# High and low halves turned by one DMA, a head pair's query and key loaded together, row maxima split before they are turned

## The chip, the cores and the metric

The kernel runs on one core of a Trainium2 chip. A core has TensorE (PE; its weight loads are PEld), VectorE (DVE), ScalarE (ACT), GpSimd (POOL) and SyncE (SP), which here issues every DMA; sixteen DMA engines move the data. The metric is the device time of one execution in microseconds, as a median of several executions.

## The reference

Two layers, each an attention with a compressed memory over four segments, and an MLP with a spatial gate. B = 1, S = 2048, D = 640, 32 heads of 20, segments of 512, MLP width 864:

```
def attention(x, wq, wk, wv, wo, beta):        # per head; g = sigmoid(beta)
    for s in range(4):
        p = softmax(q[s] @ k[s].T * 20**-0.5 + causal_mask)
        a_mem = (phi(q[s]) @ M) / (phi(q[s]) @ z + 1e-6)
        o[s] = g * a_mem + (1 - g) * (p @ v[s])
        M, z = M + phi(k[s]).T @ v[s], z + phi(k[s]).sum()
    return o @ wo                              # phi(t) = t + 1 if t > 0 else exp(t)

def mlp(x, w_in, w_sp, b_sp, w_out):
    z = gelu(x @ w_in)
    z1, z2 = z[:, :864], layernorm(z[:, 864:])
    return (z1 * (w_sp @ z2 + b_sp[:, None])) @ w_out

for _ in range(2):
    x = x + attention(layernorm(x), ...)
    x = x + mlp(layernorm(x), ...)
```

## The kernel before

Precision: every operand of a large matmul is split into two 16-bit parts, high (h) and low (l, the rest), and a product is h·h + h·l + l·h. TensorE wants its stationary operand with the contraction on the partitions, so most operands are turned: a DMA transpose turns a tile of 128 rows, one for h and one for l.

A layer has three stages. **phase1a** is attention. **phase1b** takes each of the 16 row tiles (128 rows) through the output projection (where attention has not done it already), the layer norm and both halves of w_in. **phase2** takes each of 16 row tiles of w_sp: `rows` scales and splits it and turns it, `spatial` multiplies it with z2 (96 matmuls at L380), gates, and splits and turns the result u, `tail` multiplies that with w_out (L409).

phase1a handles 64 pairs of heads (16 pairs in each of 4 segments), three slots of time for each. TensorE's order there is written out by hand: `run` goes through the slots and calls, in this order, `fetch`, `combine`, `scores`, the posted small work, `pvs`, `maxes`, `cast`, and then the dense work that is due (`value`, `unit`, `project`, `update`, `read`). The order of the other engines and of the SP queue is set by a scheduler, which goes by its own estimates; each engine, and the SP queue, then works strictly in its order.

What the change touches, in the order in which a pair meets it:

- `prep` loads a row tile, normalises it, and `split_t` (L217) makes h on ScalarE and l (here on GpSimd) and turns each, L222 and L223, into the tiles xth and xtl.
- `unit` computes the query and key rows of 128 columns; `out` splits them, and `stack` (L764, L765) writes them to DRAM, query and key in tensors of their own (stq, stk), each with three rows per dimension (h, l and one of them again). `keys` turns the key features (pkh, pkl, L701) for `update`.
- `fetch` (L777) loads a pair, four slots ahead of its scores by LF and two pairs by LM: query rows into one of five tiles qs, key rows into one of five kb, for each of two heads, four DMAs a pair.
- `scores` multiplies keys and queries twice. First, two pairs ahead, with queries as rows (mp), only to find each row's maximum (L831, `mx`, 128 x 2 x 4); later with keys as rows (es), from which ScalarE makes the exponentials P (L824). es and mp each have one buffer in PSUM, so the next es waits for P and the next mp for mx.
- `maxes` brings the maximum of each row into the query tile, as two more rows of its contraction: TensorE turns mx (L850, mtp, 32-bit), ScalarE scales it to 16 bits (L852, rows 0 to 7 of mr), VectorE takes the rest (L854, rows 32 to 39), and four DMAs (L859) write one row each. mtp lies in the pool "ms" with one buffer, which `update` (mup, L747 to L749) and `read` (num, L720, L724) use too: they wait until mtp's last reader is done.
- `combine` writes the outputs of a unit as h and l to DRAM (L904); `load_o` (L615) and phase1b's `load` (L262) load and turn them.

## Time and profile before

| | us |
|---|---|
| median of 3 runs | 2553.9 (2552.26 to 2554.67) |
| the profiled execution's own time | 2549.18 |
| its span | 2547.5 |

The profile's page gives this busy time over the whole span:

```profile
PE 2272.7 (89%) x21706; PEld 1365.3 (54%) x21706; DVE 1480.9 (58%) x2806; ACT 1146.8 (45%) x1398; POOL 903.1 (35%) x713
```

and in 40 slices of 63.7 us, in tenths, TensorE's, VectorE's, ScalarE's and GpSimd's busy share:

```profile
PE   4778787889899989999978878879998999999998
...
DVE  8677777677654454444335776767775544444431
ACT  4367676677643232211124766657774322112210
POOL 2166566678621000000023666757775110000000
```

Slices 1 to 11 and 21 to 31 are the two attentions: there all four engines work side by side. Behind them TensorE is at nine tenths or more nearly throughout. A row of a group of instructions reads: line, engine, operation, output<-inputs, shapes, count | busy us, mean ns | idle us before them and who ended it. "SPq" is SyncE's queue of DMA issues.

### The profile page before, as it was taken

To read this page: it belongs to the slowest core of one execution; us is meant where nothing else is said; L and a number is where in the kernel's file an instruction comes from. 1 tells how busy PE (TensorE), PEld (TensorE's weight loads), DVE (VectorE), ACT (ScalarE), POOL (GpSimd) and SP (SyncE) were. 2 spreads that over 40 slices of the span, in tenths; PEclk is the share of its full clock that TensorE was granted. 3 is DMA by queue.
4 is the path that set the end of the run, shared out by engine and by line. 5 is a ranking of instruction groups with operands and counts; after the bars stand their busy time and mean duration, and the time that the engine had idled before them with its cause. 6 is when DMAs were issued, how large, how long until landed. Compare 5 with 4: busy or idle time off the path is not lost. (4 is left out here: it accounts for less than half of the span.)

```text
span 2547.5 us, 53964 instructions
## 1 busy us (share of the span) xinstructions
PE 2272.7 (89%) x21706; PEld 1365.3 (54%) x21706; DVE 1480.9 (58%) x2806; ACT 1146.8 (45%) x1398; POOL 903.1 (35%) x713
## 2 busy tenths in 40 slices
PE   4778787889899989999978878879998999999998
PEld 2345454656555545555544445546565555555555
DVE  8677777677654454444335776767775544444431
ACT  4367676677643232211124766657774322112210
POOL 2166566678621000000023666757775110000000
PEclk9899899999999999999989999989999999999999
DMA  6533554323565397767542343343346335776652
GB/s 182 167 106 95 149 132 100 92 77 103 137 175 108 98 263 196 163 155 168 118 95 80 86 104 91 87 104 83 89 108 166 104 87 147 194 178 168 147 139 68
DMA packets 522189, 325.28 MB, mean 128 GB/s; under 512 B 423057, under 2 KB 468241, under 8 KB 516817
## 3 DMA queue, kind: packets, MB, share of 16 engines
q1 hardware_dynamic: 521936, 321.82, 50.1%
q8 instruction: 170, 2.79, 0.4%
q14 instruction: 83, 0.67, 0.1%
HBM read 148.26 MB, written 85.34 MB: 92 GB/s over the span
## 5 line engine op out<-in xcount | busy, mean ns | idle before, releaser
L842 POOL TENSOR_TENSOR PL<-P,PH 128x1280 f16<-128x1280 f32 x248 | 650.9, 2626 | 359.4 <-ACT PH L841 320.9
L831 DVE TENSOR_REDUCE mx<-mp 128x2 f32<-128x1024 f32 (+3 forms) x512 | 409.5, 821 | 181.4 <-PE mp L787 177.8
L824 ACT ACTIVATE P<-es,sc 128x1024 f32<-128x1024 f32 (+1 forms) x384 | 371.6, 968 | 270.2 <-PE mp L787 244.3
L841 ACT CAST PH<-P 128x1280 f16<-128x1280 f32 x256 | 321.2, 1255 | 9.6 <-PE pv L873 2.4
L380 PEld LDWEIGHTS <-wth 128*128 128x128 f16 x2048 | 200.4, 98 | 178.9 <-DMA wth<-wnh 7.9
L380 PE MATMUL gp<-zh,wth 128*128 128x432 f16 x1024 | 271.0, 346 | 7.5 <-DMA wth<-wnh 7.5
L380 PE MATMUL gp<-zh,wtl 128*128 128x432 f16 x1024 | 270.6, 346 | 1.1 <-DMA wtl<-wnl 1.1
L380 PE MATMUL gp<-zl,wth 128*128 128x432 f16 x1024 | 270.9, 346 | 0.0
L815 PE MATMUL es<-qs,kb 64*128 64x512 f16 (+3 forms) x1024 | 150.0, 311 | 70.7 <-ACT P L824 50.9
L383 ACT ACTIVATE u<-gp,bsp,un 128x864 f32<-128x864 f32 x32 | 34.2, 1070 | 391.5 <-PE gp L380 389.8
L208 POOL TENSOR_TENSOR lnrs<-lnve,mhalf 128x1 f32<-128x1 f32 x96 | 58.5, 617 | 427.9 <-DVE lnve L207 404.5
L396 POOL MEMSET unh<- 128x32 f16 x32 | 4.0, 125 | 548.4 <-DMA uh<-unh 513.9
L815 PE MATMUL mp<-kb,qs 60*128 60x512 f16 (+3 forms) x1024 | 144.8, 307 | 50.5 <-DVE mx L831 47.2
L298 PEld LDWEIGHTS <-th 128*128 128x128 f16 x1280 | 125.2, 98 | 109.2 <-DMA th<-xnh 1.4
L356 DVE TENSOR_REDUCE am<-wr 128x1 f32<-128x2048 f32 x32 | 73.2, 2286 | 169.9 <-DMA wr<-in_B_w_sp_dram 169.9
L873 PE MATMUL pv<-vs,PH 128*128 128x41 f16 x2560 | 169.7, 184 | 0.0
L873 PE MATMUL pv<-vs,PL 128*128 128x41 f16 x2560 | 166.0, 182 | 1.6 <-POOL PL L842 1.6
L815 PEld LDWEIGHTS <-kb 64*128 64x128 f16 x1024 | 48.9, 94 | 213.9 <-issue 188.3
L787 PEld LDWEIGHTS <-big 64*128 64x128 f16 x4096 | 142.0, 96 | 39.9 <-issue 5.0
L873 PEld LDWEIGHTS <-PH 128*128 128x128 f16 x2560 | 142.8, 97 | 21.1 <-ACT PH L841 0.2
L366 ACT ACTIVATE wnh<-wr,ivw 128x1024 f16<-128x1024 f32 x64 | 72.0, 1145 | 176.4 <-DVE ivw L361 104.7
L380 PEld LDWEIGHTS <-wtl 128*128 128x128 f16 x1024 | 100.0, 98 | 88.1 <-DMA wtl<-wnl 1.8
(197 smaller groups left out, 4891.0 us busy)
## 6 DMA issues: line engine op xcount, KB each, us to landing
wr<-in_B_w_sp_dram SPq DMA_DIRECT2D x32, 1024.0 KB
x<-x SPq DMA_DIRECT2D x56, 320.0 KB
qs<-stq SPq DMA_DIRECT2D x256, 60.0 KB
kb<-stk SPq DMA_DIRECT2D x256, 60.0 KB
z<-z SPq DMA_DIRECT2D x32, 432.0 KB
cz<-z SPq DMA_DIRECT2D x32, 432.0 KB
xt<-in_A_x_dram SPq DMA_DIRECT2D x32, 320.0 KB
stq<-qhl SPq DMA_DIRECT2D x40, 256.0 KB
```

The costliest lines, as they stand in the source:

```text
L208: nc.gpsimd.tensor_tensor(rs, ve, g.mhalf, ALU.pow)
L298: nc.tensor.matmul(zp[:, n, :FHH], a[:, k, :], b[:, k, c:c + FHH], start=(k == 0 and j == 0), stop=(k == KD - 1 and j == 2))
L356: nc.vector.tensor_reduce(am, wr, AX.X, ALU.max, apply_absolute_value=True)
L366: nc.scalar.activation(hn, wr[:, c], AF.Identity, scale=ivw)
L380: nc.tensor.matmul(gp[:, n, :FHH], a[:, k, :], b[:, k, n * FHH:(n + 1) * FHH], start=(k == 0 and j == 0), stop=(k == NT - 1 and j == 2))
L787: nc.tensor.matmul(out[:, o + c.start:o + c.stop], g.big[r, 64 - 64 * s:192 - 64 * s], g.mask[nm][r, m], start=False, stop=s == 1, skip_gr ...
L815: nc.tensor.matmul(out[:, h, o:o + w], a[r, ac], b[r, bc], start=o == 0, stop=False, skip_group_check=True)
L824: nc.scalar.activation(P[:, :, 512 * c:512 * c + ew], es[:, :, :ew], AF.Exp, scale=g.esc)
L831: nc.vector.tensor_reduce(self.mx[m][:, :, i], mp[:, :, o:o + w], AX.X, ALU.max)
L841: nc.scalar.copy(PH, P[:, h])
L842: (nc.gpsimd if h == 0 or n < self.N - self.TAIL else nc.vector).tensor_tensor(PL, P[:, h], PH, ALU.subtract)
L873: nc.tensor.matmul(pv[:, i, h, :], x[:, c:c + 128], v[:, j, h0 + h, :], start=(j == 0 and x is PH), stop=(j == i and x is PL), skip_group_ ...
```

## The change

Wherever h and l were two tiles and two transposes, they are one tile with a dimension of two and one transpose of twice the columns: in `split_t`, `keys`, `load_o`, `load`, phase2's `rows` and `spatial`. The outputs lie in DRAM as (row, h/l, column), so that both can be turned by one DMA. Query and key rows lie in one DRAM tensor, side by side in each row, and one tile qk holds both: `fetch` issues one DMA a head. VectorE splits the maxima into h and l (mh, 16 columns) right after the last reduction of a pair; TensorE turns both with one 16-bit matmul against a 16-bit identity; ScalarE copies the 16 rows; two DMAs write two rows each.

```
-def split_t(g, h, l, th, tl, src, low=None):
+def split_t(g, hl, t, src, low=None):
-    nc.scalar.copy(h, src)
-    (low or nc.vector).tensor_tensor(l, src, h, ALU.subtract)
-    nc.sync.dma_start(th, h, transpose=True)
-    nc.sync.dma_start(tl, l, transpose=True)
+    nc.scalar.copy(hl[:, 0], src)
+    (low or nc.vector).tensor_tensor(hl[:, 1], src, hl[:, 0], ALU.subtract)
+    nc.sync.dma_start(t.rearrange("p i k c -> p (i k) c"), hl.rearrange("p i c -> p (i c)"), transpose=True)
...
-                for o, n in ((wth, hn), (wtl, ln)):
-                    nc.sync.dma_start(o[:, 8 * i:8 * i + 8, :], n, transpose=True)
+                nc.sync.dma_start(wt[:, i].rearrange("p l k c -> p (l k) c"), hl.rearrange("p l c -> p (l c)"), transpose=True)
...
-            for o, n in ((uh, hn), (ul, ln)):
-                nc.gpsimd.memset(n[:, FH:], 0.0)
-                nc.sync.dma_start(o, n, transpose=True)
+            nc.gpsimd.memset(hl[:, :, FH:], 0.0)
+            nc.sync.dma_start(ut.rearrange("p l k c -> p (l k) c"), hl.rearrange("p l c -> p (l c)"), transpose=True)
...
+    g.ident16 = cp.tile([128, 128], F16, tag="ident16", name="ident16")
+    nc.vector.tensor_copy(g.ident16, g.ident)
...
-        for i in range(2):
-            nc.sync.dma_start(o[:, i], self.o_d[i][t // 4][(t % 4) * 128:(t % 4 + 1) * 128, :], transpose=True)
+        d = self.o_d[t // 4][(t % 4) * 128:(t % 4 + 1) * 128]
+        nc.sync.dma_start(o.rearrange("p i k c -> p (i k) c"), d.rearrange("p i c -> p (i c)"), transpose=True)
...
-            self.pk = [self.u1.tile([128, 4, 128], F16, tag="pk" + p, name="pk" + p) for p in "hl"]
-            for i, o in enumerate(self.pk):
-                nc.sync.dma_start(o, hl[:, i], transpose=True)
+            self.pk = self.u1.tile([128, 2, 4, 128], F16, tag="pk", name="pk")
+            nc.sync.dma_start(self.pk.rearrange("p i t c -> p (i t) c"), hl.rearrange("p i c -> p (i c)"), transpose=True)
...
-        rows = self.st[nm][s % 2][128 * m:128 * m + 128]
+        rows = self.st[s % 2][128 * m:128 * m + 128, :, i]
...
-        for nm, t in (("q", self.qs[n % self.NQ]), ("k", self.kb[n % self.NK])):
-            d = self.st[nm][n // 16 % 2]
-            for h in range(2):
-                c = 40 * (n % 16) + 20 * h
-                self.nc.sync.dma_start(t[64 * h:64 * h + 60], d[c:c + 20].rearrange("p l c -> (p l) c"))
+        for h in range(2):
+            c = 40 * (n % 16) + 20 * h
+            self.nc.sync.dma_start(self.qk[n % self.NQK][64 * h:64 * h + 60], self.st[n // 16 % 2][c:c + 20].rearrange("p l i c -> (p l) i c"))
...
             for i, o, w in red:
                 nc.vector.tensor_reduce(self.mx[m][:, :, i], mp[:, :, o:o + w], AX.X, ALU.max)
+            if c == 2:
+                mx = self.mx[m]
+                mh = self.mh[m] = self.pl2.tile([128, 2, 2, 4], F16, tag="mh", name="mh")
+                nc.vector.tensor_scalar(mh[:, :, 0], mx, -1.0 / MS, None, ALU.mult)
+                nc.vector.scalar_tensor_tensor(mh[:, :, 1], mx, -1.0 / MS, mh[:, :, 0], ALU.mult, ALU.subtract)
...
-        nc.tensor.transpose(tp, mx.rearrange("p h i -> p (h i)"), g.ident)
-        mr = self.pl2.tile([40, 128], F16, tag="mr", name="mr")
-        nc.scalar.mul(mr[0:8], tp, -1.0 / MS)
-
-        nc.vector.scalar_tensor_tensor(mr[32:40], tp, -1.0 / MS, mr[0:8], ALU.mult, ALU.subtract)
-        q = self.qs[n % self.NQ]
-        for i in range(2):
-            for h in range(2):
-                r = 64 * h + 60 + i
-                nc.sync.dma_start(q[r:r + 1, :].rearrange("o (t c) -> o t c", t=4), mr[32 * i + 4 * h:32 * i + 4 * h + 4])
+        tp = self.pm.tile([128, 512], F32, tag="ms", name="mtp")[:16, :128]
+        nc.tensor.matmul(tp, self.mh.pop(n).rearrange("p h i t -> p (h i t)"), g.ident16, start=True, stop=True)
+        mr = self.pl2.tile([16, 128], F16, tag="mr", name="mr")
+        nc.scalar.copy(mr, tp)
+        for h in range(2):
+            r = 64 * h + 60
+            nc.sync.dma_start(self.qk[n % self.NQK][r:r + 2, 0].rearrange("i (t c) -> i t c", t=4), mr[8 * h:8 * h + 8])
```

The SP queue in layer 0's attention, about two pairs where the last outputs of segment 2 (4x160) are written; qs and kb are query and key tiles, o the outputs that are loaded and turned. Before:

```order
L859 DMA qs_347<-mr 1x4x128 x4
L777 DMA qs_351<-stq 60x512 x2
L904 DMA oh_2<-ohl 128x4x160
L777 DMA kb_356<-stk 60x512 x2
L904 DMA ol_2<-ohl 128x4x160
L615 DMA_TRANSPOSE o<-oh_1 128x5x128
L859 DMA qs_348<-mr 1x4x128 x4
L641 DMA x_0_3<-x_9465 128x640
L777 DMA qs_347<-stq 60x512 x2
L777 DMA kb_352<-stk 60x512 x2
L615 DMA_TRANSPOSE o<-ol_1 128x5x128
```

The same place of the changed kernel:

```order
L855 DMA qk_349<-mr 2x4x128 x2
L772 DMA qk_353<-st 60x1024 x2
L900 DMA o_2<-ohl 128x4x160 x2
L613 DMA_TRANSPOSE o<-o_1 128x10x128
L855 DMA qk_350<-mr 2x4x128 x2
L639 DMA x_0_3<-x_9307 128x640
L772 DMA qk_349<-st 60x1024 x2
```

The order is the same; 21 issues became 12.

VectorE in the same attention, one pair's three slots; mx are the reductions (of the slots one, two, one), mr<-mtp the second reader of the turned maxima, ohl and x the outputs and the projection. Before:

```order
L698 SCALAR_TENSOR_TENSOR phl<-phk,sc,phl 128x512
L639 SCALAR_TENSOR_TENSOR x_6015<-yps,sc,xt 128x320
L831 TENSOR_REDUCE mx<-mp 128x2
L901 SCALAR_TENSOR_TENSOR ohl<-oat,ohl 128x480
L831 TENSOR_REDUCE mx<-mp 128x2
L884 TENSOR_TENSOR rs<-pv,iomg 128x8
L639 SCALAR_TENSOR_TENSOR x_6015<-yps,sc,xt 128x320
L885 RECIPROCAL rs<-rs 128x8
L889 TENSOR_TENSOR ab<-pv,rs 128x328
L854 SCALAR_TENSOR_TENSOR mr<-mtp,mr 8x128
L831 TENSOR_REDUCE mx<-mp 128x2 x2
```

The same place of the changed kernel:

```order
L696 SCALAR_TENSOR_TENSOR phl<-phk,sc,phl 128x512
L637 SCALAR_TENSOR_TENSOR x_5911<-yps,sc,xt 128x320
L826 TENSOR_REDUCE mx<-mp 128x2
L830 TENSOR_SCALAR mh<-mx 128x2x4
L831 SCALAR_TENSOR_TENSOR mh<-mx,mh 128x2x4
L897 SCALAR_TENSOR_TENSOR ohl<-oat,ohl 128x480
L826 TENSOR_REDUCE mx<-mp 128x2
L880 TENSOR_TENSOR rs<-pv,iomg 128x8
L637 SCALAR_TENSOR_TENSOR x_5911<-yps,sc,xt 128x320
L881 RECIPROCAL rs<-rs 128x8
L885 TENSOR_TENSOR ab<-pv,rs 128x328
L826 TENSOR_REDUCE mx<-mp 128x2 x2
```

The read of mtp behind ab is gone; two operations stand right behind the pair's last reduction, which mtp now waits for.

A third place, one pair later on VectorE in the changed kernel, where the statistics of a loaded row tile (lnst<-xt) come between:

```order
L826 TENSOR_REDUCE mx<-mp 128x2
L205 BN_STATS lnst<-xt 128x6 x2
L830 TENSOR_SCALAR mh<-mx 128x2x4
L206 BN_AGGR lnmv<-lnst 128x2
L831 SCALAR_TENSOR_TENSOR mh<-mx,mh 128x2x4
L207 TENSOR_SCALAR lnve<-lnmv 128x1
```

Over the program, of the 128 pairs 75 have nothing between the last reduction and the second of these two operations, 33 one operation, and 20 two to five.

More of the change, by code (lines that the diff above doesn't have):

```diff
@@ L284, in xn_t @@
         def xn_t(xn):
-            th = pe2.tile([128, KD, 128], F16, tag="th", name="th")
-            tl = pe2.tile([128, KD, 128], F16, tag="tl", name="tl")
-            h, l = [pe1.tile([128, D], F16, tag="xn" + p, name="xn" + p) for p in "hl"]
-            split_t(g, h, l, th, tl, xn)
-            return th, tl
+            th = pe2.tile([128, 2, KD, 128], F16, tag="th", name="th")
+            hl = pe1.tile([128, 2, D], F16, tag="xnhl", name="xnhl")
+            split_t(g, hl, th, xn)
+            return th[:, 0], th[:, 1]
         def w_in_half(i, th, tl):
@@ L377, in spatial @@
             for k in range(NT):
[L378 removed]
+                for j, (a, b) in enumerate(((0, zh), (0, zl), (1, zh))):
                     for n in range(2):
[L380 removed]
+                        nc.tensor.matmul(gp[:, n, :FHH], wt[:, k // 8, a, k % 8, :], b[:, k, n * FHH:(n + 1) * FHH],
                                          start=(k == 0 and j == 0), stop=(k == NT - 1 and j == 2))
@@ L509 @@
 class Attention:
-    NQ = NK = 5
+    NQK = 5
     LM = 2
@@ L551, in setup @@
         self.po = pool("apo", 1, space=PSUM)
-        self.qs = [sk.tile([128, L], F16, name=f"qs{i}") for i in range(self.NQ)]
-        self.kb = [sk.tile([128, L], F16, name=f"kb{i}") for i in range(self.NK)]
+        self.qk = [sk.tile([128, 2, L], F16, name=f"qk{i}") for i in range(self.NQK)]
         self.vs = [p.tile([128, 4, H, 2 * DH + 1], F16, name=f"vs{i}") for i, p in enumerate((av, sk))]
@@ L740, in update @@
         g, nc = self.g, self.nc
-        pkh, pkl = self.pk
+        pkh, pkl = self.pk[:, 0], self.pk[:, 1]
         n = len(TH[m])
@@ L1063, in rows @@
         return [a[0, t * 128:(t + 1) * 128, :] for t in range(NT)]
-    g.st = {n: [dram(f"st{n}{i}", (D, 3, L), F16) for i in range(2)] for n in "qk"}
+    g.st = [dram(f"st{i}", (D, 3, 2, L), F16) for i in range(2)]
     x = rows(x)
@@ L1068, in interleaved_layers @@
         i = f"_{layer}"
-        o_d = [[dram(f"o{p}{i}_{n}", (L, D), F16) for n in range(NSEG)] for p in "hl"]
+        o_d = [dram(f"o{i}_{n}", (L, 2, D), F16) for n in range(NSEG)]
         x1_d = [dram(f"x1{i}_{t}", (128, D)) for t in range(NT)]
```

62 lines of the change are left out of this document (30 added, 32 removed).

## The prediction

> **What bounds the kernel now.** I read the windows first (the span cut into the stages of both layers), then TensorE's waits, then the chain that ended last, then single pairs in the timeline. The columns of the windows are the length, then busy time of each engine with its instructions, the granted clock, the DMA share and GB/s.
>
> ```profile
> span 2547.5 us, 53964 instructions
> ```
>
> ```profile
> 31.00:717.00 686.00, 571.93 (x7557) 360.54 (x7558) 490.39 (x934) 441.73 (x563) 423.46 (x277) 0.93 0.45 118
> 717.00:908.00 191.00, 189.38 (x1069) 104.36 (x1068) 97.93 (x197) 61.33 (x69) 18.71 (x29) 1.00 0.55 137
> 908.00:1298.00 390.00, 381.06 (x2252) 220.29 (x2251) 168.12 (x293) 75.64 (x74) 11.87 (x41) 0.99 0.71 171
> 1298.00:1962.00 664.00, 554.07 (x7511) 352.27 (x7510) 446.50 (x843) 431.21 (x546) 416.05 (x273) 0.94 0.38 98
> 1962.00:2134.00 172.00, 172.00 (x983) 95.66 (x980) 81.22 (x171) 49.79 (x57) 18.37 (x29) 1.00 0.40 104
> 2134.00:2547.00 413.00, 399.88 (x2333) 229.06 (x2330) 168.10 (x291) 74.22 (x71) 5.58 (x35) 0.99 0.64 152
> ```
>
> The rows are attention, first MLP half (phase1b) and second (phase2) of layer 0, then the same of layer 1. Outside attention TensorE is full: it idles 1.6, 8.9, 0 and 13.1 us there, so transposes and loads that get cheaper in those stages gain almost nothing. In attention it idles 114 and 110 us, and no engine is full. TensorE's order there is written out by hand, so each wait delays all behind it. The whole run's waits of TensorE (total, times, longest):
>
> ```profile
> PE es L815 <- ACT P L824: 50.9, 71, 3.8
> PE mp L815 <- DVE mx L831: 47.2, 43, 3.2
> PE mup L747 <- DVE mr L854: 36.7, 22, 4.6
> PE num L720 <- DVE mr L854: 26.0, 27, 3.2
> PE es L815 <- DMA qs<-mr: 18.2, 21, 3.2
> ```
>
> Three of the five belong to the row maxima: 62.7 us wait until VectorE's L854 has read the turned maxima and the one "ms" bank is free, 18.2 us until the DMAs of L859 have put them into the query tile. The chain that ended last, in attention of layer 1, has the same names among its costs, and L859's issues on the SP queue beside them:
>
> ```profile
> by line: issue 6.7%; DVE mx L831 5.3%; PE kps L661 5.2%; PE pv L873 5.1%; ACT PH L841 4.8%; PE qps L661 4.5%; PE es L815 4.1%; DMA qs<-mr 3.8%; PE vps L600 3.7%; ACT P L824 3.7%; PE num L720 3.1%; PE mp L815 3.0%; PE yps L633 2.9%; POOL PL
> ```
>
> 3.8% of 626 us are 24 us for the landing of the maxima in one layer.
>
> **The maxima, the largest part.** Two places show what goes. In the first, rows of ACT, DVE, TensorE and the SP queue:
>
> ```profile
> 416.83 0.27 PE L850 MATMUL mtp<-ident,mx 128*8 128x128 f32 x1
> 416.94 0.38 PE L661 MATMUL qps<-xth,wql 128*128 128x512 f16 x1
> 417.15 0.38 PE L661 MATMUL kps<-xth,wkh 128*128 128x512 f16 x1
> ...
> 423.16 0.28 PE L747 MATMUL mup<-vs,pkh 128*128 128x147 f16 x1 [4.58 <-DVE mr L854]
> ```
>
> ```profile
> 418.61 0.26 ACT L852 ACTIVATE mr<-mtp 8x128 f16<-8x128 f32 x1
> ```
>
> ```profile
> 421.21 0.89 DVE L205 BATCH_NORM_STATS2 lnst<-xt 128x6 f32<-128x320 f32 x2 [3.48 <-DMA xt<-in_A_x_dram]
> ...
> 422.82 0.28 DVE L854 SCALAR_TENSOR_TENSOR mr<-mtp,mr 8x128 f16<-8x128 f32 x1
> 423.13 0.96 DVE L831 TENSOR_REDUCE mx<-mp 128x2 f32<-128x768 f32 x1
> ```
>
> ```profile
> 423.06 2.53 SPq L859 DMA_DIRECT2D qs<-mr  x4
> ```
>
> ScalarE had read the bank by 418.87; VectorE stood on a load and read it at 422.82 to 423.10. After the change ScalarE is the bank's only reader, so the update of memory would start 4.2 us sooner. But the same VectorE queue holds the maximum at 423.13, which TensorE needs a slot later: a long wait is mostly moved, not removed. The short waits, where VectorE is only the 0.28 us and a handover behind ScalarE, have less of that behind them. Bounds: at least 0.31 us for each of the 49 waits, 15 us; at most all 62.7 us. **I take 30**, nearer the lower end because of rows like 423.13.
>
> The four DMAs take 2.53 us of the SP queue (0.63 each); the last of two leaves 1.3 us sooner, and the first starts with ScalarE's end, at least 0.31 us sooner. The 21 waits of 18.2 us average 0.87 us, less than 1.6, so most vanish; bounds 0 (if two-row writes land later by as much) and 18.2: **15**.
>
> The Trainium skill, DMA: Bandwidth & Descriptors, section "Why a DMA increments its semaphore by 16 and not by 1", says that a DMA runs on the largest number up to 16 that divides the slowest dimension of both sides. By it a write of two rows from eight partitions uses two of the DMA engines where one row from four used four, and the 15 would shrink by what the longer landing takes; no row of before shows such a write.
>
> TensorE's own turn, its readers and two of VectorE's smallest operations:
>
> ```profile
> L854 DVE SCALAR_TENSOR_TENSOR mr<-mtp,mr 8x128 f16<-8x128 f32 x128 | 35.8, 280 | 19.9 <-ACT mr L852 16.2 <-DMA qs<-stq 1.1
> L850 PE MATMUL mtp<-ident,mx 128*8 128x128 f32 x128 | 35.3, 276 | 0.0
> ...
> L884 DVE TENSOR_TENSOR rs<-pv,iomg 128x8 f32<-128x8 f32 x128 | 20.0, 156 | 12.9 <-PE pv L873 12.9
> ```
>
> The next matmul starts 0.11 us after mtp (416.83 to 416.94); the 16-bit matmul of 512 columns behind it holds the array 0.21 us (to 417.15), so one of 128 should hold it 0.05: 128 x 0.05 = **6 us** saved, bounds 0 and 14. The Trainium skill, Perfetto Trace Analysis, section "Transposes", speaks against this edit: logical transposes should be transposes, not standard matmuls, which the new mtp is. By that rule the 6 us would be 0 or a small loss; the trace has no such matmul against an identity to set beside it.
>
> VectorE loses 128 x 0.28 = 36 us and the 16.2 us in which L854 stood for ScalarE, and gets 256 small operations at 0.15 to 0.28 us: 38 to 72 us. Net work between 2 and 36 us more over both layers, of which VectorE's share of the chain (its row L831 is 5.3%) passes on a little; against that stand the 16.2 us. I set both at **0**, bounds -5 and +5.
>
> **The queue.** Durations of issues, min/median/max in ns:
>
> ```profile
> L777 SPq DMA_DIRECT2D qs<-stq x256: 320/373/1593, 68.4 to 1908.3; - x128
> L777 SPq DMA_DIRECT2D kb<-stk x256: 315/397/1811, 72.7 to 1913.5; - x128
> ```
>
> ```profile
> L222 SPq DMA_TRANSPOSE xth<-xnhl x32: 1202/1228/2148, 28.9 to 1736.1; - x32
> ```
>
> ```profile
> L369 SPq DMA_TRANSPOSE wth<-wnh x64: 1232/1301/4417, 903.3 to 2482.3; - x64
> ```
>
> Five 128-column blocks cost 1.23 us to issue and eight 1.30, so nearly all is fixed and a joint issue of ten should cost 1.2 to 1.4 (at worst twice 1.23). In attention the change drops 256 loads at 0.39 us (100 us of queue) and one of each pair of transposes: 32 of xt, 30 of the features, 24 of the outputs, 86 x 1.2 = 103 us; with 256 maxima DMAs at 0.63, 161 us, some 360 us in the two stages leave a queue that had 1350 us. Little of it ends a wait of TensorE directly beside the 18.2 us counted: what loads and transposes give by starting sooner I take as **8 us**, bounds 0 and 30.
>
> **What it adds.** A joint transpose can't start before its low part is there, and lands as a whole. At the start and the end nothing covers that:
>
> ```profile
> 28.85 1.32 SPq L222 DMA_TRANSPOSE xth<-xnhl  x1
> 30.98 1.21 SPq L223 DMA_TRANSPOSE xtl<-xnhl  x1
> ```
>
> ```profile
> 31.59 0.45 PE L600 MATMUL vps<-wvh,xth 128*128 128x320 f16 x1 [6.02 <-DMA xth<-xnhl]
> ```
>
> ```profile
> 2531.95 1.23 SPq L397 DMA_TRANSPOSE uh<-unh  x1
> 2533.34 1.22 SPq L397 DMA_TRANSPOSE ul<-unl  x1
> ```
>
> ```profile
> 2534.93 0.45 PE L409 MATMUL cyp<-wuh,uh 128*128 128x320 f16 x2 [2.85 <-DMA uh<-unh]
> 2535.21 0.43 PE L409 MATMUL cyp<-wul,uh 128*128 128x320 f16 x2
> 2536.31 0.31 PE L409 MATMUL cyp<-wuh,ul 128*128 128x320 f16 x1 [0.66 <-DMA ul<-unl]
> ```
>
> At the end a transpose lands 2.98 us after its issue begins. The joint one begins when the low part is ready, at the latest 2533.34, and its second half costs up to 1.38 us more (the distance of the two landings): 2537.2 instead of 2536.31, with four matmuls more behind it, 1.4 us. The first tile of attention and the first features in each layer should lose as much: five places, **6 us lost**, bounds 2 and 12.
>
> mtp now waits for two operations of VectorE behind the last maximum, and its queue decides when they run. In before there is room:
>
> ```profile
> 1508.59 0.68 DVE L831 TENSOR_REDUCE mx<-mp 128x2 f32<-128x512 f32 x1
> ```
>
> ```profile
> 1510.44 0.27 PE L850 MATMUL mtp<-ident,mx 128*8 128x128 f32 x1
> ```
>
> From 1509.27 to 1510.44 are 1.17 us, against some 0.35 for the two. Where the order puts nothing or one operation between (108 of 128 pairs), no wait. In 20 pairs two to five stand between, up to the statistics of a row tile, which wait for a load (the third place of the order). What is queued behind mtp on TensorE is the dense work, so such a wait costs in full: 20 x 0.3 = **6 us lost**, bounds 0 and 30.
>
> The memsets, the 16-bit identity and the stores with 1 KB runs instead of 2 KB are hidden: phase2's TensorE is full, and the next reader of a store is a slot or more behind.
>
> **Sum.** 30 + 15 + 6 + 0 + 8 - 6 - 6 = 47 us off TensorE's waits. TensorE that comes sooner meets ScalarE's and VectorE's score work sooner: their rows (50.9 and 47.2 us) are as large as what goes. By the windows ScalarE and VectorE are busy 64% to 71% of attention, so I give back a little over a third: 17. **30 us faster.** The profiled execution took 2549.2 us, its span and 1.7 around it, and would take 2519; it lay 4.7 below the median of the runs, 2553.9, so the median comes to **2524**.
>
> **Rivals.** *Most of it is realised.* If the waits behind L854 go without coming back and VectorE's freedom from ScalarE (16.2 us) and the shorter queue spare the stalls on loads too, 62.7 + 18.2 + 6 + 8 - 12 = 83 us at most: 2471 to 2504. For it: three rows of five have one cause. Against: row 423.13. *Moved, not removed.* The waits reappear at es and mp, whose two rows could take all of 47 us: within 5 us of 2554. For it: maximum and exponential are ready only one slot ahead. Against: over half of the 49 waits are short. *Slower: mtp behind VectorE's queue.* If the two operations come late not in 20 pairs but in the 53 with anything between, at 1.2 us (a reduction or a statistics step, 0.9, and the handovers), 64 us are lost against 47 gained, 17 slower: 2560 to 2575. It decides from 0.9 us a pair on. Against it: 1.17 us of room in the rows above. *The joint transpose is no cheaper to issue*, 2.5 us instead of 1.2, so the queue gives nothing and mr's DMAs stand behind it: 10 us faster, 2544.
>
> **Chances.** Forecast 0.48 (its own range 2504 to 2546), realised 0.22, moved 0.12, slower 0.14, no cheaper issue 0.04. A measurement of this kernel can tell about 0.2%, 5 us, from no change. Faster by more: 0.74; within: 0.12; slower: 0.14. The range leaves out the last tenth on each side: 2476 to 2559.
>
> **What would show it.** mup and num should wait for ScalarE's mr, in under 20 us; es for the qk DMA in under 5; mtp should have an idle time near 0 (above 10 us the slower rival is at work); DMA_TRANSPOSE issues of ten blocks at 1.2 to 1.4 us; TensorE's idle in the attention windows near 95 us each instead of 114 and 110; es and mp waits a little above 98 us together. If these rows don't move and the time does, the cause is elsewhere in VectorE's new order, and this account is wrong.

## The result and the profile after

| | runs | median, us | lowest to highest | against before (95% interval) |
|---|---|---|---|---|
| before | 4 | 2553.3 | 2552.3 to 2554.7 | |
| after | 4 | 2509.9 | 2506.1 to 2524.8 | 0.984 (0.980 to 0.9881) |

The change makes the kernel 43.5 us (1.7%) faster; 2524 was forecast. The profiled executions, on which all that follows rests, took 2549.2 and 2510.1 us: 39.1 less.

First TensorE's waits in the changed kernel (total, times, longest), the rows that answer to those of before and the new ones:

```profile
PE mp L810 <- DVE mx L826: 47.6, 42, 3.5
PE mtp L850 <- DVE mh L831: 40.7, 20, 3.7
PE es L810 <- ACT P L819: 37.8, 61, 1.9
...
PE mup L744 <- DMA pk<-phl: 12.2, 4, 5.7
...
PE mup L744 <- ACT mr L852: 6.1, 14, 1.2
...
PE es L810 <- DMA qk<-mr: 3.4, 3, 2.5
...
PE num L717 <- ACT mr L852: 1.9, 6, 0.3
```

The waits of mup and num for the bank are 8.0 us instead of 62.7, those of es for the maxima's DMA 3.4 instead of 18.2. A new one stands second: mtp waits 40.7 us for the split on VectorE, in 20 places of 2 us. The windows over the two attention stages (length, busy time of PE, PEld, DVE, ACT and POOL with instructions, granted clock, DMA share, GB/s):

```profile
35.00:705.00 670.00, 569.31 (x7559) 355.13 (x7558) 516.14 (x982) 440.53 (x560) 423.28 (x277) 0.94 0.46 120
...
1276.00:1924.00 648.00, 564.20 (x7602) 356.61 (x7600) 469.25 (x917) 433.63 (x549) 418.43 (x277) 0.95 0.41 104
```

Both are shorter, 687 to 671 and 676 to 648 us (stage by stage from the first vps matmul to the first of the MLP); the MLP stages are as long as before within 2.2 us each. VectorE got busier, TensorE idles less and its clock is a hundredth higher. The small operations of the maxima, by shape:

```profile
L831 DVE SCALAR_TENSOR_TENSOR mh<-mx,mh 128x8 f16<-128x8 f32 x128 | 48.9, 382 | 3.7
...
L830 DVE TENSOR_SCALAR mh<-mx 128x8 f16<-128x8 f32 x128 | 41.4, 323 | 2.7
...
L852 ACT CAST mr<-mtp 16x128 f16<-16x128 f32 x128 | 32.0, 250 | 16.2 <-PE mtp L850 16.2
...
L850 PE MATMUL mtp<-ident,mh 128*16 128x128 f16 x128 | 29.1, 227 | 40.7 <-DVE mh L831 40.7
...
L880 DVE TENSOR_TENSOR rs<-pv,iomg 128x8 f32<-128x8 f32 x128 | 19.8, 155 | 6.0 <-PE pv L869 6.0
```

The split operations average 382 and 323 ns, over the 0.28 us that the prediction took as the most. The view of the tile mh says why a mean misleads here (ns: shortest, median, longest):

```profile
L830 DVE TENSOR_SCALAR mh<-mx x128: 150/172/2600, 105.5 to 1902.1; 128x8 f16<-128x8 f32 x128
L831 DVE SCALAR_TENSOR_TENSOR mh<-mx,mh x128: 107/167/2581, 105.7 to 1902.8; 128x8 f16<-128x8 f32 x128
```

Their median is 0.17 us, but 20 of the 256 last over 0.8 us, the longest 2.6. One of the long ones in the timeline (start, duration, engine, line, operation, and the idle time before it):

```profile
565.09 2.61 POOL L842 TENSOR_TENSOR PL<-P,PH 128x1280 f16<-128x1280 f32 x1 [1.17 <-ACT PH L841]
...
565.14 2.58 DVE L831 SCALAR_TENSOR_TENSOR mh<-mx,mh 128x8 f16<-128x8 f32 x1
...
567.65 1.21 DVE L826 TENSOR_REDUCE mx<-mp 128x2 f32<-128x1024 f32 x1
567.78 0.22 PE L850 MATMUL mtp<-ident,mh 128*16 128x128 f16 x1 [2.02 <-DVE mh L831]
```

GpSimd's subtraction begins at 565.09 and ends at 567.70; the eight elements on VectorE, begun 0.05 us later, end at 567.72. TensorE stands 2.02 us for them. Of the 128 low-part operations, the 96 that no GpSimd operation overlaps average 165 ns, the other 32 average 1035 ns. The durations above the medians add up to 47 us, in which by these ends VectorE stands still. Of the 20 waits of mtp, 18 are for a split whose two operations together ran 0.5 to 3.5 us over their medians. An estimate from these rows, the lesser of wait and excess in each place, puts 34 of the 40.7 us down to that. No run moved GpSimd's work elsewhere: that it is the cause is read from the ends, which fall together.

Issues on the SP queue (count, shortest/median/longest in ns):

```profile
L772 SPq DMA_DIRECT2D qk<-st x256: 320/349/2229, 75.5 to 1872.2; - x128
```

```profile
L855 SPq DMA_DIRECT2D qk<-mr x256: 610/617/1193, 107.6 to 1906.9; - x128
```

```profile
L222 SPq DMA_TRANSPOSE xt<-xnhl x32: 1252/1362/2512, 31.2 to 1698.1; - x32
```

A joint issue of ten blocks takes 1.36 us where two of five took 1.23 each; a joint load takes no longer than a single one did.

### The profile page after: what moved, and what is told of

It reads as the page before. It is cut to its first block, busy times and chain, and to the rows that moved or that the text cites. A ratio compares the mean times of both kernels' runs of the same rounds, so it can differ in the third digit from the quotient of the medians.

```text
span 2508.3 us, 52442 instructions
## 1 busy us (share of the span) xinstructions
PE 2268.5 (90%) x21706; PEld 1356.3 (54%) x21706; DVE 1528.8 (61%) x2935; ACT 1147.4 (46%) x1398; POOL 899.8 (36%) x681
## 5 line engine op out<-in xcount | busy, mean ns | idle before, releaser
L377 PE MATMUL gp<-zh,wt 128*128 128x432 f16 x2048 | 465.9, 348 | 10.1 <-DMA wt<-wn 10.1
L377 PEld LDWEIGHTS <-wt 128*128 128x128 f16 x3072 | 301.6, 98 | 271.3 <-DMA wt<-wn 10.9
L377 PE MATMUL gp<-zl,wt 128*128 128x432 f16 x1024 | 272.3, 348 | 0.0
L810 PEld LDWEIGHTS <-qk 64*128 64x128 f16 (+1 forms) x2048 | 80.1, 96 | 259.7 <-issue 200.0
L354 DVE TENSOR_REDUCE am<-wr 128x1 f32<-128x2048 f32 x32 | 73.1, 2286 | 212.4 <-DMA wr<-in_B_w_sp_dram 212.4
L598 PE MATMUL vps<-wvh,xt 128*128 128x320 f16 x640 | 160.7, 320 | 30.6 <-DVE vs L604 10.7
L810 PE MATMUL mp<-qk 60*128 60x512 f16 (+3 forms) x1024 | 140.1, 309 | 48.0 <-DVE mx L826 47.6
L810 PE MATMUL es<-qk 64*128 64x512 f16 (+3 forms) x1024 | 141.0, 311 | 42.1 <-ACT P L819 37.8
L406 PE MATMUL cyp<-wuh,ut 128*128 128x320 f16 (+1 forms) x896 | 166.6, 303 | 9.2 <-DMA ut<-un 8.5
L406 PEld LDWEIGHTS <-ut 128*128 128x128 f16 (+1 forms) x1344 | 132.7, 99 | 66.6 <-DMA ut<-un 10.7
L364 ACT ACTIVATE wn<-wr,ivw 128x1024 f16<-128x1024 f32 x64 | 71.9, 1143 | 187.5 <-DVE ivw L359 106.0
```

Of the source, the lines that this page charges most:

```text
L354: nc.vector.tensor_reduce(am, wr, AX.X, ALU.max, apply_absolute_value=True)
L377: nc.tensor.matmul(gp[:, n, :FHH], wt[:, k // 8, a, k % 8, :], b[:, k, n * FHH:(n + 1) * FHH], start=(k == 0 and j == 0), stop=(k == NT - ...
L406: nc.tensor.matmul(yp[:, n, :320], a[:kn[k], k, :], b[:kn[k], k, n * 320:(n + 1) * 320], start=(k == 0 and j == 0), stop=(k == KO - 1 and ...
L598: nc.tensor.matmul(ps, a[:, k, c], b[:, k, n * 320:(n + 1) * 320], start=(i == 0), stop=(i == 14))
L810: nc.tensor.matmul(out[:, h, o:o + w], a[r, ac], b[r, bc], start=o == 0, stop=False, skip_group_check=True)
```

## Where the 39 us are

Two things turned out to add up. The clock records of the trace give TensorE stretches at half rate, in whole multiples of 3.41 us. Cutting attention of the kernel before and of the changed one at those multiples, and counting TensorE's idle time in each piece that begins in attention and runs at full rate:

```
idle time in 3.41 us     pieces at full rate, and how many have a next piece at half rate
                         before          after
under 1.25 us            282, 0          291, 0
1.25 to 1.5              15, 2           9, 0
1.5 to 2.0               23, 12          21, 12
2.0 and more             24, 24          18, 18
```

In all 14 kernels together it is 307 of 309 from 2.0 us on, 183 of 333 from 1.5, 9 of 185 from 1.25 and none of 4004 below. So two microseconds of waiting close together cost their own length and up to half of the 3.41 us behind them (up to, because TensorE idles in some of that time as well: 26.9 of 184.3 us before). With this, attention's length can be split into idle time, half the half-rate time, and a remainder that lies between 1038 and 1060 in all 14 kernels (us, both layers; eight of them):

```
               attention   idle   half-rate/2   remainder
before            1362.8  224.1          92.2      1046.6
after             1318.3  184.8          76.8      1056.7
joins_only        1360.8  232.1          90.5      1038.3
maxes_only        1354.3  199.5          99.0      1055.7
mh_first          1342.2  202.0          90.5      1049.8
mtp_late          1314.0  203.7          63.1      1047.2
mh_spare          1396.8  228.3         114.3      1054.2
low_on_pe         1423.6  278.2          88.7      1056.7
```

Of the 44.4 us that attention lost, 39.2 are idle time and 15.4 the clock by this count; the remainder took back 10.2, so that the time in which TensorE is busy fell by 5.2 only. Outside attention 5.3 us were lost, 3.1 of them before the first matmul.

## The experiments

The mean granted clock of every run is on record, not only of the profiled ones. As the granted rate is one or a half in every trace, a run's span times what its mean clock lacks to 1 is the time that it lost at half rate. The last two columns split the mean span of the runs so; the standard errors are 1.2 to 4.5 us of the first and 0.7 to 2.3 us of the second. The 17 runs of before are those made beside joins_only.

| kernel | runs | median, us | against before (95% interval) | lost at half rate, us | rest, us |
|---|---|---|---|---|---|
| before | 17 | 2552.1 | | 93.9 | 2455.6 |
| after | 4 | 2509.9 | 0.984 (0.980 to 0.9881) | 86.6 | 2424.2 |
| joins_only | 12 | 2546.0 | 0.9985 (0.9969 to 1.0001) | 96.5 | 2448.7 |
| maxes_only | 6 | 2536.0 | 0.9935 (0.9912 to 0.9957) | 105.6 | 2428.6 |
| mh_first | 6 | 2530.4 | 0.9911 (0.9889 to 0.9934) | 100.7 | 2426.7 |
| mh_flat | 5 | 2514.5 | 0.9849 (0.9828 to 0.9871) | 86.4 | 2425.2 |
| fetch_apart | 6 | 2520.9 | 0.989 (0.9868 to 0.9911) | 93.2 | 2425.9 |
| turns_apart | 5 | 2518.5 | 0.9872 (0.9851 to 0.9893) | 93.6 | 2421.3 |
| mtp_late | 6 | 2508.2 | 0.9835 (0.9811 to 0.9859) | 73.1 | 2431.8 |
| mtp_turn | 6 | 2508.3 | 0.9847 (0.9822 to 0.9871) | 85.3 | 2423.0 |
| rows_four | 6 | 2524.3 | 0.9912 (0.9886 to 0.9938) | 85.0 | 2439.2 |
| mh_spare | 6 | 2583.0 | 1.0126 (1.0099 to 1.0153) | 117.8 | 2461.9 |
| split_act | 6 | 2684.7 | 1.0517 (1.0487 to 1.0546) | 122.8 | 2556.5 |
| low_on_pe | 5 | 2613.4 | 1.0254 (1.0231 to 1.0277) | 99.2 | 2512.1 |

### The halves: joint parts alone, maxima alone

joins_only is the changed kernel with the maxima of before; maxes_only is the kernel before with the new maxima.

```diff
-        nc.tensor.matmul(tp, self.mh.pop(n).rearrange("p h i t -> p (h i t)"), g.ident16, start=True, stop=True)
+        nc.tensor.transpose(tp, mx.rearrange("p h i -> p (h i)"), g.ident)
...
+        nc.vector.scalar_tensor_tensor(mr[32:40], tp, -1.0 / MS, mr[0:8], ALU.mult, ALU.subtract)
```

> The changed kernel with the maxima as before: mx is turned in 32 bits, VectorE reads the turned maxima again, four DMAs write one row each. Joint transposes and the joint query and key load stay. If the gain is that of the maxima (the bank freed by ScalarE, two DMAs fewer), TensorE's waits for mr stay near 60 us and for the DMA of the maxima near 15 us, and the time is 2535 to 2553 us. If it is that of the shorter SP queue, it is 2505 to 2525 us and the waits for DMAs go.

> The kernel before with the new maxima alone (split on VectorE, turned in 16 bits, two DMAs of two rows); every transpose and load apart as before. Theory of the maxima: 2505 to 2525 us, mup and num wait under 15 us for mr, mtp waits some 30 to 45 us for mh. Theory of the SP queue: 2540 us or more.

By the ratio, the joint parts alone give 4 us (0 to 8), which is not clear of no change; the maxima alone 17 us (11 to 22); both 41 (30 to 51). TensorE's waits with the joint parts alone:

```profile
PE es L810 <- ACT P L819: 60.2, 74, 3.9
PE mp L810 <- DVE mx L826: 52.4, 43, 3.3
PE mup L744 <- DVE mr L849: 37.6, 25, 4.1
PE num L717 <- DVE mr L849: 25.5, 27, 3.5
...
PE es L810 <- DMA qk<-mr: 7.3, 12, 2.8
```

The wait for the maxima's DMA falls by 11 us through the shorter queue alone, and es for ScalarE takes 9 of them. With the maxima alone:

```profile
PE mtp L857 <- DVE mh L838: 38.8, 18, 5.6
...
PE mup L749 <- ACT mr L859: 8.3, 12, 2.2
...
PE es L817 <- DMA qs<-mr: 4.6, 2, 4.1
...
PE num L722 <- ACT mr L859: 1.9, 6, 0.3
```

The bank's wait goes with the maxima alone: by these rows the theory of the maxima holds, by the time neither does. Neither half gives what both do. The last two columns of the table say where that lies. The rest adds up: it falls by 6.9 and by 27.0 us alone, by 31.4 together. The clock does not: 2.6 and 11.7 us more are lost at half rate alone, 7.3 fewer together (with four runs, the standard error of the changed kernel's 86.6 is 4.4). So the some 20 us that appear only in company are in the clock.

### Which joint part, in the company of the new maxima

Loads apart again, and transposes apart again, each in the changed kernel:

```diff
-            self.nc.sync.dma_start(self.qk[n % self.NQK][64 * h:64 * h + 60], self.st[n // 16 % 2][c:c + 20].rearrange("p l i c -> (p l) i c"))
+            for i in range(2):
+                self.nc.sync.dma_start(self.qk[n % self.NQK][64 * h:64 * h + 60, i], self.st[n // 16 % 2][c:c + 20, :, i].rearrange("p l c -> (p l) c"))
```

```diff
-    nc.sync.dma_start(t.rearrange("p i k c -> p (i k) c"), hl.rearrange("p i c -> p (i c)"), transpose=True)
+    for i in range(2):
+        nc.sync.dma_start(t[:, i], hl[:, i], transpose=True)
```

> The changed kernel with four loads of 60 rows for a pair of heads again (query and key rows by themselves, from the joint store layout) instead of two. Maxima and joint transposes stay as changed. The joint parts alone gave 6 us, the new maxima alone 17, both together 43: some 20 us appear only in company, and this run and the one with transposes apart ask which joint part brings them. Theory Q (the queue that issues the loads is what the company relieves, and its 256 loads at 0.37 us, 95 us of issue, stand ahead of the maxima's writes and of the transposes): 8 to 20 us slower than the changed kernel, 2518 to 2530, the wait of es for the maxima's DMA above 8 us (3.4 now). Theory T (the transposes bring it): within 5 us of 2510. Theory K (what appears in company is the granted clock: fewer windows at half rate): either time, but with half-rate time in attention near 150 us if the time stays (154 now), near 180 if it goes up.

> The changed kernel with a DMA transposition for each of the H and L parts again, at all six places. Maxima and joint loads stay as changed. Theory T (86 issues of 1.2 us less in attention, and their landings, bring the 20 us that appear only in company): 10 to 20 us slower than the changed kernel, 2520 to 2530, waits of vps, mup or es for DMAs up by as much. Theory Q (the loads bring it): within 5 us of 2510, or some us faster, since high parts land sooner again (the five places of the prediction: 6 us). Theory K: time and half-rate time in attention (154 us now) move together, whichever way.

By the medians the joint loads are worth 11 us here and the joint transposes 9, both with intervals that overlap that of the changed kernel: neither is clear of the noise. What difference there is lies in the clock, as theory K has it: 93.2 and 93.6 us lost at half rate against 86.6, and a rest of 2425.9 and 2421.3 against 2424.2. The profiled executions, of which that of fetch_apart is the slowest of its six, have 181 and 188 us of half-rate time in attention against 154. The rows that theories Q and T named hardly moved: with the loads apart es waits 4.0 us for the maxima's DMA, not 8; with the transposes apart that wait is 9.7 us and vps waits 10.0 for xt (6.2 in the changed kernel), which is theory T's sign at less than its size. In turns_apart the first matmul starts 2.6 us sooner (32.1 us into the span instead of 34.7): the price of a joint transposition that nothing covers.

### The layout of the split, and its place in VectorE's order

mh_flat lays the high and low parts apart, so that each operation writes eight elements in a row; mh_first holds VectorE's later-written work behind the split.

```diff
-                mh = self.mh[m] = self.pl2.tile([128, 2, 2, 4], F16, tag="mh", name="mh")
+                mh = self.mh[m] = self.pl2.tile([128, 2, 8], F16, tag="mh", name="mh")
```

```diff
+                if self.split is not None:
+                    behind.enter_context(self.tc.issue_after(self.split.ins))
```

> The changed kernel with the split maxima laid out so that each of the two operations writes eight neighbouring elements (h and l apart) and each DMA writes the h rows or the l rows of both heads. If the layout (runs of four elements) makes the operations 323 and 382 ns long, they fall to 150 to 220 ns and VectorE is busy some 40 us less; the time falls by 0 to 8 us. If a 16-bit result or the dependence on the operation just ahead does, they stay within 40 ns of that and the time within 4 us of 2510.

> The changed kernel with one thing else: VectorE's work that is written after the split of the maxima is queued behind it, so that two or more operations stand between the last reduction and the split in 5 pairs instead of 20. If mtp's waits (40.7 us) cost in full, they fall to 10 to 15 us and the time to 2478 to 2492 us. If such a wait only stands for one that would come at es or mp, those two rise by 20 us or more and the time stays within 6 us of 2510.

The layout changes nothing: 278 and 351 ns a piece on average, with medians of 171 and 168 ns where they were 172 and 167, and the same time. The order was a miss: the kernel is 20 us slower than the changed one, 14 of them lost at half rate. Its waits:

```profile
PE es L810 <- ACT P L819: 46.4, 65, 4.0
PE mp L810 <- DVE mx L826: 34.9, 32, 3.3
PE mup L744 <- DMA pk<-phl: 23.6, 7, 4.4
PE mtp L850 <- DVE gm L730: 20.9, 12, 3.9
PE vps L598 <- DVE vs L604: 19.1, 6, 8.5
```

mtp no longer waits for the split (4.2 us) but 20.9 for gm, another reader of the same bank, which now stands behind the split; vs and the DMA of pk are late too.

### The turn later in TensorE's order

```diff
-                if h == 1 and c == 0 and 0 <= n - 1 + self.LM < N:
-                    self.maxes(n - 1 + self.LM)
...
             until(t + 1)
+            if c == 0 and 0 <= n - 1 + self.LM < N:
+                self.maxes(n - 1 + self.LM)
```

> The changed kernel with the turn of the maxima (mtp, its copy to mr and the two row writes) written behind the dense matmuls of its slot instead of ahead of them; nothing else moves. VectorE gets some 2 us more for the split before TensorE asks for it. In the changed kernel 20 turns wait 40.7 us for the split. Theory W (these waits cost in full, the earlier remedy only moved them to the other readers of the bank because it held VectorE's other work back): mtp's wait under 10 us, the kernel 20 to 35 us faster than the changed one, 2475 to 2490. Theory M (the pair's chain of maxima, exponential and cast is what sets the pace, a wait is taken by whoever comes first): mtp's wait goes but es, mp, mup and num take it up, within 8 us of 2510. A later write of the rows should show in es for the maxima's DMA: below 8 us if there is slack of a slot, 20 or more if not.

```profile
PE mp L810 <- DVE mx L826: 65.3, 54, 4.4
PE es L810 <- ACT P L819: 49.5, 69, 2.8
...
PE num L717 <- ACT mr L852: 11.8, 18, 2.8
...
PE mup L744 <- ACT mr L852: 11.0, 16, 1.4
...
PE mtp L850 <- DVE mh L831: 9.6, 10, 1.8
```

mtp's wait falls by 31 us and the time stays: theory M. mp takes up 18, es 12, num and mup 15; the idle sum rises by 19. In its place half-rate time falls from 154 to 126 us, since many short waits replaced a few of 2 us: 13.7 us of clock pay for most of it (over all runs 73.1 us are lost at half rate, against 86.6).

### TensorE's form of the turn

```diff
-        nc.tensor.matmul(tp, self.mh.pop(n).rearrange("p h i t -> p (h i t)"), g.ident16, start=True, stop=True)
+        nc.tensor.transpose(tp, self.mh.pop(n).rearrange("p h i t -> p (h i t)"), g.ident16)
```

> The changed kernel with the turn of the maxima as a transposition on TensorE (16-bit result in the bank) instead of a matmul against the identity. The prediction gave 6 us (0 to 14) to the 16-bit matmul against the 32-bit transposition of before; the Trainium skill's Perfetto Trace Analysis, section Transposes, says a transposition should be used. Theory of the prediction: both 16-bit forms hold the array as long (0.05 us), mtp's rows stay at 227 ns within 20 and the time within 4 us of 2510. Theory of the rule: rows shorter than 227 ns and some us faster, 2500 to 2506. ScalarE's copy from a 16-bit bank may differ by some 20 ns of 250, off the path.

The rows last 226 ns instead of 227, the time is the same. The rule of the Trainium skill's Perfetto Trace Analysis, section "Transposes", is neither borne out nor contradicted here: for 16 rows of 16 bits the two forms cost alike.

### The maxima's DMAs

```diff
-            nc.sync.dma_start(self.qk[n % self.NQK][r:r + 2, 0].rearrange("i (t c) -> i t c", t=4), mr[8 * h:8 * h + 8])
+            for i in range(2):
+                r = 64 * h + 60 + i
+                nc.sync.dma_start(self.qk[n % self.NQK][r:r + 1, 0].rearrange("o (t c) -> o t c", t=4), mr[8 * h + 4 * i:8 * h + 4 * i + 4])
```

> The changed kernel with the maxima written by four DMAs of one row each, instead of two of two rows; all else as changed. It prices the term of the prediction on the maxima's DMAs (15 us with the earlier start, of which some 1.3 us for each late landing is the second pair of issues). Theory of the prediction: es's wait for the maxima's DMA up from 3.4 to between 8 and 15 us, the kernel 4 to 12 us slower than the changed one. Theory M (a wait that goes is taken up by the next): es for the DMA up, but the time within 4 us of 2510. By the Trainium skill's rule on the number of engines a DMA runs on (DMA: Bandwidth & Descriptors, Why a DMA increments its semaphore by 16 and not by 1) a single row lands sooner after its issue than two: the medians from issue to landing say whether that is so.

14 us slower than the changed kernel, all of it in the rest and not in the clock, but not where either theory looked: es waits 4.2 us for the maxima's DMA, hardly more than 3.4.

```profile
PE mp L810 <- DVE mx L826: 61.9, 45, 3.4
PE es L810 <- ACT P L819: 48.7, 65, 3.9
PE mtp L850 <- DVE mh L831: 30.0, 16, 3.7
```

So the earlier start and the shorter queue are enough for that wait to go (the latter alone brings it to 7.3 in joins_only), without the write of two rows. mp waits 14 us more and es 11 more for ScalarE, mtp 11 less; how 256 more issues of 0.6 us bring that about stays open. No run shows when these writes land. So what the prediction drew from the Trainium skill, DMA: Bandwidth & Descriptors, section "Why a DMA increments its semaphore by 16 and not by 1", that fewer engines land later, is not decided; the page gives the number of engines.

### The price of VectorE's time

mh_spare adds two dead operations per pair a slot ahead of the split; split_act gives the high part to ScalarE, with the later turn of mtp_late.

```diff
+            if c == 1:
+                sp = self.pl2.tile([128, 2, 2, 2], F16, tag="spare", name="spare")
+                mx = self.mx[m][:, :, 2:4]
+                nc.vector.tensor_scalar(sp[:, :, 0], mx, -1.0 / MS, None, ALU.mult)
+                nc.vector.scalar_tensor_tensor(sp[:, :, 1], mx, -1.0 / MS, sp[:, :, 0], ALU.mult, ALU.subtract)
```

```diff
-                nc.vector.tensor_scalar(mh[:, :, 0], mx, -1.0 / MS, None, ALU.mult)
+                nc.scalar.mul(mh[:, :, 0], mx, -1.0 / MS)
```

> The changed kernel with two more small operations on VectorE per pair of heads, written a slot ahead of the split: the same two operations on half of the maxima, into a tile that nobody reads. 256 operations of some 0.25 us, 60 to 70 us more for VectorE; nothing waits for them. It prices what the prediction set at 0 (-5 to 5): VectorE's own work. Theory V (VectorE sets much of attention's pace, and TensorE's waits are where it shows): 20 us or more slower than the changed kernel, 2530 and up, with mp's and mtp's waits up together. Theory M (the pace is set by no single engine, and small work falls into VectorE's idle time, 130 us of it before the maxima alone): 0 to 10 us slower, 2510 to 2520. Theory of the prediction (0): within 5 us of 2510.

> The changed kernel with the turn of the maxima behind its slot's dense work (as in the run mtp_late, 2508) and the high part of the split on ScalarE instead of VectorE: 128 operations of 0.32 us, 41 us, less for VectorE, some 30 us more for ScalarE and one handover more, for which the later turn leaves room. Theory V (VectorE's work sets the pace): 10 to 20 us faster than mtp_late, 2488 to 2498. Theory M (no single engine does): within 6 us of 2508, VectorE's gain given back where es waits for ScalarE's exponential. If the handover is late, mtp's wait goes above 20 us again (9.6 in mtp_late).

The dead work costs 73 us, 31 of them lost at half rate; mtp's wait rises from 40.7 to 70.6 us and mp's from 47.6 to 57.9. Its rows:

```profile
L830 DVE TENSOR_SCALAR spare<-mx 128x4 f16<-128x4 f32 x128 | 82.2, 643 | 0.0
...
L831 DVE SCALAR_TENSOR_TENSOR spare<-mx,spare 128x4 f16<-128x4 f32 x128 | 39.5, 309 | 2.7
```

They are 122 us instead of the 60 to 70 expected, because they too stand behind GpSimd: where no GpSimd operation overlaps, they average 155 and 157 ns, which would be 40 us for all 256. The first has half the elements of the split's first operation and lasts twice as long on average: what is measured is mostly the time behind GpSimd, not the work. Theory V holds by its numbers (2530 and up, mp's and mtp's waits up). split_act was to relieve VectorE and is 175 us slower than the changed kernel:

```profile
L831 DVE SCALAR_TENSOR_TENSOR mh<-mx,mh 128x8 f16<-128x8 f32 x128 | 268.7, 2099 | 90.2 <-ACT mh L830 89.8
```

VectorE stands 90 us for ScalarE, and then starts just after GpSimd has begun: 110 of its 128 operations overlap GpSimd's, and the median one lasts 2.57 us. Fewer operations, 178 us more of VectorE's time than both took in the changed kernel (268.7 against 90.3).

### The split without VectorE

```diff
+        nc.tensor.matmul(tp, mx.rearrange("p h i -> p (h i)"), g.ident, start=True, stop=False, is_transpose=True, skip_group_check=True)
+        nc.scalar.mul(mr[0:8], tp, -1.0 / MS)
...
+        nc.tensor.matmul(tp, g.ident16[:8, :8], mr[0:8], start=False, stop=True, skip_group_check=True)
+        nc.scalar.mul(mr[32:40], tp, -1.0 / MS)
```

> The changed kernel with the split of the maxima taken off VectorE: TensorE turns the 32-bit maxima straight after the last maximum, ScalarE makes the high row from the bank, a second small matmul (behind the slot's dense work) adds the high row times 16384 onto the bank, and ScalarE makes the low row from what is left. Each part is written by one DMA for both heads. VectorE loses both split operations, 90 us busy in the changed kernel, of which some 48 us are operations that lasted up to 2.6 us instead of 0.165 because a subtraction of GpSimd was under way; TensorE gains 128 small matmuls, ScalarE 128 operations of 0.26 us. Theory L (operations of VectorE that read and write SBUF alone stand still while GpSimd works, and VectorE's time is what attention's pace hangs on; two such operations more, 122 us, cost 73 us, 0.6 us for each): 40 to 60 us faster than the changed kernel, 2450 to 2470, mtp's waits under 5 us, mp's well below 48. Theory M (TensorE's waits only change places): within 10 us of 2510, a new wait of the second matmul for ScalarE's mr of 20 us or more, or of mup and num for the bank (8 now, 63 before the change).

A miss: 104 us slower than the changed kernel. The second matmul waits for ScalarE in 121 of 128 pairs:

```profile
PE mtp L859 <- ACT mr L848: 142.3, 121, 5.6
PE mp L811 <- DVE mx L827: 62.0, 43, 4.3
PE es L811 <- ACT P L820: 16.8, 36, 2.5
```

VectorE is busy 58 us less in attention and waits more for TensorE instead (its reductions 255 us instead of 132). This is theory M's new wait, but it was not exchanged against others: TensorE's idle time in attention rose by 93 us. A wait met in nearly every pair costs; one met in 20 of 128 was made up elsewhere. Whether VectorE's freedom is worth the 40 to 60 us is not decided, since no run had it without a new wait. No kernel beat the changed one beyond its interval; mtp_late and mtp_turn equal it.

## Why the prediction was right, and where it was not

**The bank and its readers** (30, bounds 15 to 62.7). The waits of mup and num fell by 54.7 us: right in mechanism, 25 too small. What row 423.13 was to stand for did not hold these waits back.

**The maxima's DMA** (15). 14.8 us of its wait went. But rows_four shows that the two-row write is not why, and that four writes cost 14 us elsewhere.

**The 16-bit turn** (6). The rows fell from 276 to 227 ns, 128 of them 6.3 us (the prediction's own figures, 0.11 and 0.05, would give 7.7). That the time followed was not tested; the other 16-bit form is no different.

**VectorE's own work** (0, from -5 to 5) and **mtp behind the split** (6 lost). These are the steps that failed, and in one place: "256 small operations at 0.15 to 0.28 us: 38 to 72 us". They took 90.3. The count of late pairs was right, 20 waits, 16 of them with two or more other operations between, but each cost 2.0 us, not 0.3, 40.7 in all: the term was mis-sized by 35. The slower rival was at work with fewer pairs and a higher price than it was given. Most of both comes from the 47 us in which the split stands behind GpSimd; mh_spare gives what such time costs, 73 us for 122, by which rate 47 would cost 28, an estimate. The trace of before had a row that shows it, in an operation whose operands also all lie in SBUF:

```profile
L698 DVE SCALAR_TENSOR_TENSOR phl<-phk,sc,phl x30: 733/778/2987, 73.2 to 1729.8; 128x512 f16<-128x512 f32 x30
```

The prediction took its price from L854 and L884, which read PSUM and never stretch: 122 of the 128 of L854 overlap an operation of GpSimd, and all last 279 to 282 ns.

**The queue** (8, bounds 0 to 30). 11 us for the loads and 9 for the transposes by the medians, within the bounds, but neither clear of the noise and both in the clock. The issue's length was right (1.36 us).

**Uncovered transposes** (6 lost, bounds 2 to 12). At the start 3.1 us later; at the end one wait of 4.8 us where 2.85 and 0.66 stood, 1.3 more, as priced there (the 2537.2 of that sum should read 2537.7; its 1.4 is right). mup waits 5.5 us longer for pk (12.2 after; 6.7 before, L747 and L749 together). That is 9.9: more than taken, within the bounds.

**Given back to es and mp** (17 lost). Wrong in sign: es fell by 13.1, mp stayed. The giving back was at mtp.

Together: 54.7 + 14.8 + 13.1 - 0.4 for mp - 40.7 - 5.5 for pk are 36.0 us of waits; the idle time in attention fell by 39.2. The prediction had 30, and 95 us of idle in each attention window; they are 101 and 84, 92 on average. That the sum came so near is luck: the bank is 25 too small and the giving back 30 off, mtp is 35 off the other way, and the 6 of the turn and the 8 of the queue have no row among the waits. No term held the clock. By the medians 14 us lie between forecast and result. Over all runs the clock gave 7 us and the rest 31; that it makes up the 14 is not shown.

What stays open: why the clock loses less when the joint parts and the new maxima come together, and more with either alone. The exchange of waits in joins_only (11 for 9) is seen, its rule isn't.

## What to carry to other kernels

Before work is moved to an engine, look at the longest as well as the mean of operations of the same kind there, with operands in the same memory; here a factor of four between median and longest was another engine's doing. A wait of TensorE that appears in a few places can be exchanged for others without any change in time, so judge a remedy by the sum of all waits and by the clock, not by the row that it removes. A handover that every iteration has to wait for is a different thing: low_on_pe, where it was met in 121 of 128 pairs, lost 104 us. And a change of 10 us that lies in the clock needs more runs than one that lies in the rest.

## What was not expected of the hardware

VectorE's operations of the kinds tensor_scalar and scalar_tensor_tensor whose operands all lie in SBUF can stand still while GpSimd subtracts: the split takes 0.17 us alone, up to 2.6 us beside it, ending about 0.02 us after GpSimd's operation. Those that read the PSUM bank (L854 of before, 0.28 us; the khl rows, 0.68) do not stretch. Nor does everything in SBUF: in the changed kernel 90 reciprocals of rs overlap GpSimd and none is over 0.21 us, and 39 statistics of a loaded row tile (lnst<-xt) and none is over 0.50. The Trainium skill, SBUF — State Buffer, section "Who interferes with whom", says that an operation of VectorE with two inputs in SBUF, or in a two-port mode, shares a port pair with GpSimd and that whoever comes first holds it for the whole instruction; the trace agrees (2.58 us at 565.14, behind the 2.61 us at 565.09).

TensorE's clock falls to half for the next 3.41 us after 2 us of idle time within 3.41 us (42 of 42 pieces in the kernels before and after), about half the time from 1.5 us on (24 of 44), and never below 1.25 (573 pieces). The Trainium skill, TensorE: Matmul & The Clock Gate, section "Part 1: The HAM clock gate (the "warmup" mystery)", gives an idle window of about 3.4 us as the condition; the window's length agrees, but here 2 us of idle in it were enough.
